# The second half of an ELU layer, recast in the form of the expert stage that follows it

## The chip, the cores and the metric

One core of one Trainium2 chip runs the whole kernel. The metric is device time in microseconds: the median of three runs before the change is 1423.83 us (1423.03 to 1424.04).

## The reference

Three layers follow each other on 2304 tokens of 512 numbers.

1. Linear attention over 4 batches x 8 heads x 576 tokens: features `exp(p)` and `exp(-p)` of a projection from which the largest absolute value was taken, two small matrix products, a division.
2. A feed-forward layer with ELU. Its inputs `w_in` and `w_out` come in 64-bit floating point:

```python
h = x @ w_in                                  # 512 -> 2048
g = where(h > 0, h, exp(minimum(h, 0)) - 1)
x = g @ w_out                                 # 2048 -> 512
```

3. Four experts of width 1024 on all tokens, weighted by normalised probabilities: `out += p[:, e] * (relu(x @ w1[e]) @ w2[e])`.

## The kernel before, in words

**Products.** To keep float32 precision, each factor is split into a high part and a remainder, and each product is three matmuls (high x high, high x remainder, remainder x high).

**Order of the work.** The kernel is written as Python generators that hand out instructions in program order; a planner (the tile framework, with a simulated time line) then orders each engine's instructions by program order and by when they become ready, and places the waits. A tile of a pool is waited for until all its earlier users are done. All DMAs go through SP's queue, in order.

**Attention** (lines 168 to 329) works on 16 pairs of heads, several in flight. While the ELU layer's first half runs, each `slot()` (line 718) hands out 1.4 attention steps and 2 steps of `weight_stream`. A `limit` and a `goal` keep attention some pairs ahead of the ELU token tiles.

**Weights of the ELU layer.** `convert64` (line 100) turns a 128 x 256 piece of 64-bit numbers into float32: two ScalarE passes, four VectorE passes, a GpSimd multiplication and a GpSimd addition, then the split into high part (ScalarE) and remainder (GpSimd), written to a ring of 16 tiles. There are 32 tiles of weights, 64 pieces. `conversions` (line 400) yields nothing while the ring has no room; tiles are released by the last of the nine token tiles.

**ELU layer.** `Elu` (line 512) is one unit: a token tile of 256 and two blocks of 128 hidden features. `l1` makes 24 matmuls of 256 columns, then ReLU of the negative, Exp, a combination, a copy and a subtraction; `l2`, one unit later, makes 24 matmuls into four accumulators. The 16 blocks of hidden features are done in two halves of eight: the first half runs over all nine token tiles (the last three interleaved, `TAIL`) and stores partial sums to DRAM (`x1scr`); the second half loads the tokens again from DRAM (`load_x`), loads the partial sums (`load_part`) and stores the sum (`x1fin`). Two matmuls of an unbroken queue of 24 look like this:

```python
PE.matmul(ph[:, j], w[:, 0, c], xh[:, kc], start=(kc == 0), stop=False)
PE.matmul(ph[:, j], w[:, 0, c], xl[:, kc], start=False, stop=False)
```

**Expert stage.** Tokens are taken in three groups of 2 x 384. The first product of an expert uses one level of Strassen's scheme: seven products instead of eight. `split_x1` (line 588) forms the seven token combinations, `weight_stream` (line 434 on) the seven weight combinations of each of four quarters. `Up` (line 622) has `begin`, `middle` and `end` per quarter: seven products of 6 matmuls of 384 columns, accumulated in three PSUM banks; ScalarE copies a bank (`keep`) before TensorE adds to it, VectorE adds the copies. `half` turns each of the four result blocks into a high part (ScalarE, line 653) and a remainder (VectorE, line 654). `Down` (line 685) is the second product, of 512 columns, one PSUM bank for 128 tokens; it scales and adds to sums kept in DRAM (`yscr`). One expert's weights take 14 + 8 ring tiles; the ring is 16 tiles plus 7 more (`ring2`) that are opened during the second ELU half, when the conversions are over.

## Time and profile before

| what | value |
|---|---|
| median of three runs | 1423.83 us |
| profiled execution | 1424.05 us |
| its span | 1422.3 us |
| TensorE busy | 1380.5 us, 8688 matmuls |
| VectorE / ScalarE / GpSimd busy | 698.2 / 619.9 / 446.7 us |
| granted TensorE clock, mean | 0.997 |

The span is the time from the first to the last instruction that the profiler recorded; all prices below come from this one execution. A busy TensorE need not be TensorE at its peak, since matmuls overlap: the distance from one matmul's start to the next one's tells more than a duration does. `L525` is line 525 of the kernel.

### The profile page before, as it was taken

The numbers are of one execution on the slowest core, as the hardware profiler recorded it, in microseconds if no ns is written. First come the engines' busy times: TensorE is split into PE (matmuls) and PEld (weight loads), VectorE is DVE, ScalarE is ACT, GpSimd is POOL, SyncE is SP. The second block draws the span as 40 slices with busy tenths as digits, with TensorE's granted clock in tenths as the row PEclk, the third lists the DMA queues.
The fourth block names the chain that finished last, engine by engine and source line by source line (L and its number), as shares of the span: only waits on it lengthen the run. The fifth ranks groups of instructions, "written<-read, shape, count | busy, mean of one in ns | idle before, by whom it ended". The sixth has DMA issues, their size and how long they took to land.

```text
span 1422.3 us, 22325 instructions
## 1 busy us (share of the span) xinstructions
PE 1380.5 (97%) x8688; PEld 1286.9 (90%) x8688; DVE 698.2 (49%) x1150; ACT 619.9 (44%) x1348; POOL 446.7 (31%) x499
## 2 busy tenths in 40 slices
PE   7889999999999999999999999999999999999998
PEld 6788999999988999998898989898888989899897
DVE  7998856575588534333434323234432325323332
ACT  6777776665656544343333443122421214322121
POOL 5567654434588512033102350002320004300000
PEclk9999999999999999999999999999999999999999
DMA  5433222120423345313333233434145251433421
GB/s 162 128 118 117 88 66 77 40 74 24 128 90 118 112 143 191 108 46 104 114 131 148 94 106 135 160 112 148 45 149 181 105 196 52 141 111 133 167 78 67
DMA packets 93625, 160.22 MB, mean 113 GB/s; under 512 B 28496, under 2 KB 39888, under 8 KB 93520
## 3 DMA queue, kind: packets, MB, share of 16 engines
q1 hardware_dynamic: 93520, 158.80, 33.7%
q8 instruction: 68, 1.11, 0.3%
q14 instruction: 37, 0.30, 0.1%
HBM read 109.22 MB, written 49.55 MB: 112 GB/s over the span
## 4 chain that ended last, share of the span: by engine, by line
PE 74%; DVE 11%; DMA 5%; POOL 4%; issue 3%; ACT 3%; SPq 0%; DVEq 0%; POOLq 0%; ACTq 0%
PE bank L701 8%; PE bank L702 8%; PE bank L703 8%; PE bank L642 8%; PE bank L643 7%; PE bank L644 7%; PE bank L555 3%; PE bank L556 3%; PE bank L554 3%; PE bank L527 3%; PE bank L525 3%; PE bank L526 3%; PE bank L237 2%; PE bank L316 2%; DMA wst<-in_w 2%
## 5 line engine op out<-in xcount | busy, mean ns | idle before, releaser
L701 PE MATMUL bank<-w,h 128*128 128x512 f32 x576 | 224.5, 392 | 4.0 <-ACT h L653 4.0
L642 PE MATMUL bank<-xv,w 128*128 128x384 f32 x672 | 224.3, 340 | 3.1 <-ACT cm L648 2.9
L643 PE MATMUL bank<-xv,w 128*128 128x384 f32 x672 | 226.6, 337 | 0.0
L702 PE MATMUL bank<-w,h 128*128 128x512 f32 x576 | 225.5, 392 | 0.0
L644 PE MATMUL bank<-xv,w 128*128 128x384 f32 x672 | 223.4, 338 | 0.0
L703 PE MATMUL bank<-w,h 128*128 128x512 f32 x576 | 198.3, 391 | 0.7 <-DVE h L654 0.7
L462 POOL TENSOR_TENSOR w<-wst,w 128x256 fp32r<-128x256 f32 x80 | 62.2, 796 | 341.0 <-ACT w L461 336.9
L555 PE MATMUL bank<-gl,w 128*128 128x256 f32 x576 | 162.3, 286 | 6.3 <-DVE gl L538 5.0
L556 PE MATMUL bank<-gh,w 128*128 128x256 f32 x576 | 160.9, 284 | 0.0
L554 PE MATMUL bank<-gh,w 128*128 128x256 f32 x576 | 156.3, 288 | 3.9 <-ACT gh L537 3.4
L642 PEld LDWEIGHTS bank<-xv,w 128*128 128x128 f32 x672 | 126.6, 188 | 11.1 <-ACT cm L648 3.5
L654 DVE SCALAR_TENSOR_TENSOR h<-bank,h 128x384 fp32r<-128x384 f32 x144 | 77.4, 554 | 115.1 <-ACT h L653 115.1
L653 ACT ACTIVATE h<-bank 128x384 fp32r<-128x384 f32 x144 | 66.8, 490 | 151.6 <-PE bank L644 91.7
L701 PEld LDWEIGHTS bank<-w,h 128*128 128x128 f32 x576 | 108.5, 188 | 25.1 <-ACT h L653 5.3
L643 PEld LDWEIGHTS bank<-xv,w 128*128 128x128 f32 x672 | 126.8, 189 | 4.4
L702 PEld LDWEIGHTS bank<-w,h 128*128 128x128 f32 x576 | 108.6, 189 | 20.6
L644 PEld LDWEIGHTS bank<-xv,w 128*128 128x128 f32 x672 | 126.3, 188 | 0.0
L703 PEld LDWEIGHTS bank<-w,h 128*128 128x128 f32 x576 | 107.3, 188 | 20.0 <-DVE h L654 1.6
L555 PEld LDWEIGHTS bank<-gl,w 128*128 128x128 f32 x576 | 110.1, 191 | 9.6 <-DVE gl L538 7.5
L554 PEld LDWEIGHTS bank<-gh,w 128*128 128x128 f32 x576 | 106.1, 191 | 6.8 <-ACT gh L537 6.5
L556 PEld LDWEIGHTS bank<-gh,w 128*128 128x128 f32 x576 | 110.1, 191 | 0.2
L648 ACT ACTIVATE cmab<-bank 128x384 f32<-128x384 f32 x48 | 23.6, 492 | 178.0 <-PE bank L644 178.0
(119 smaller groups left out, 2991.0 us busy)
## 6 DMA issues: line engine op xcount, KB each, us to landing
xv<-xvd SPq DMA_DIRECT2D x42, 768.0 KB, 4.4
wst<-in_w SPq DMA_DIRECT2D x64, 256.0 KB, 2.8
xvd<-xv SPq DMA_DIRECT2D x21, 768.0 KB, 4.4
yscr<-y SPq DMA_DIRECT2D x54, 256.0 KB, 2.3
y<-yscr SPq DMA_DIRECT2D x54, 256.0 KB, 2.9
w<-in_w_in SPq DMA_DIRECT2D x32, 256.0 KB, 2.8
w<-in_w_out SPq DMA_DIRECT2D x32, 256.0 KB, 3.0
kq<-in_kq SPq DMA_DIRECT2D x16, 320.0 KB, 3.0
```

The costliest lines, as they stand in the source:

```text
L462: on[WL[v % len(WL)]].tensor_tensor(out=lo, in0=x, in1=f32(hi), op=ALU.subtract)
L554: PE.matmul(o, w[:, 0, c], self.gh[:, j], start=start, stop=False)
L555: PE.matmul(o, w[:, 0, c], self.gl[:, j], start=False, stop=False)
L556: PE.matmul(o, w[:, 1, c], self.gh[:, j], start=False, stop=stop)
L642: PE.matmul(o, hi[:, c], x[:, 0, kc], start=not more and kc == 0, stop=False, skip_group_check=more)
L643: PE.matmul(o, hi[:, c], x[:, 1, kc], start=False, stop=False, skip_group_check=more)
L644: PE.matmul(o, lo[:, c], x[:, 0, kc], start=False, stop=kc == 1, skip_group_check=more)
L653: A.activation(h[:, 0], c, ACTF.Relu)
L654: V.scalar_tensor_tensor(out=h[:, 1], in0=c, scalar=0.0, in1=f32(h[:, 0]), op0=ALU.max, op1=ALU.subtract)
L701: PE.matmul(self.acc, h[:, 0, c], w[:, 0], start=f == 0, stop=False)
L702: PE.matmul(self.acc, h[:, 0, c], w[:, 1], start=False, stop=False)
L703: PE.matmul(self.acc, h[:, 1, c], w[:, 0], start=False, stop=f == 2 * NQ - 1)
```

## The change

The first half of the ELU layer stays as it is, with the last two token tiles interleaved instead of three. The second half takes the form of the expert stage, as an expert numbered -1:

- Its weights are still converted piece by piece, but right behind the first half's, and stored as float32 in DRAM (`wscr`); `weight_stream` later loads them like an expert's and forms the Strassen combinations and the splits. They take no ring tile until then.
- Its first product is `UpElu`, Strassen's scheme of `Up` with an ELU in `half`. Its tokens are loaded from DRAM in groups of 2 x 384 (`x_att`) and split by `split_x`.
- Its second product is `Out`: plain matmuls of 384 columns with the weights as the stationary operand, accumulated in four banks for 384 tokens; `drain` adds the first half's partial sums, loaded into `part` tiles, and stores to `x1fin`.
- The ring beside the main one has 6 tiles instead of 7, and pools move between the two sides of SBUF.

The diff, cut to its core:

```diff
-RING2 = 7
+RING2 = 6
...
-TAIL = 3
+TAIL = 2
+ATE = 6
+WFAST = 4
+TEB = 2
+PB = 4
+EL = 'V'
...
-    xscr = [[dram.tile([P, S], F32, name=f"xscr{b}_{p}") for p in range(NP)] for b in range(B)]
-    x1fin = [dram.tile([P, KD, TS], F32, name=f"x1fin{t}") for t in range(NTS)]
+    xscr = [dram.tile([P, NP, S], F32, name=f"xscr{b}") for b in range(B)]
+    wscr = {(nm, f): dram.tile([P, DM], F32, name=f"w{nm}{f}") for nm in ("in", "out") for f in range(FP, 2 * FP)}
+    x1fin = [[dram.tile([P, KD, TC], F32, name=f"x1fin{g}_{s}") for s in range(2)] for g in range(NG)]
...
-    p2 = ExitStack()
-    tmp = pool("tmp", stack=p2)
-    gt = pool("gt", LAG + 1, stack=p2)
...
         adder.tensor_tensor(out=f32(top), in0=f32(top), in1=low, op=ALU.add)
+        if dst.dtype == F32:
+            SP.dma_start(dst, f32(top))
+            return
         A.activation(dst[:, 0], f32(top), ACTF.Copy)
         yield
         G.tensor_tensor(out=dst[:, 1], in0=f32(top), in1=f32(dst[:, 0]), op=ALU.subtract)
...
+    tmp = pool("tmp", stack=right, side="right")
+    gt = pool("gt", LAG + 1, stack=right, side="right")
...
-        pl = ring2[0] if len(order_b) % (RING + RING2) < RING2 else ring
+        pl = ring if len(order_b) % (RING + RING2) < RING else ring2[0]
...
-        if ring2[0] is None or RING2 <= n < RING + RING2 and n - RING2 >= freed[0] - (len(users) - RING):
-            return False
-        return n - freed_b[0] < RING + RING2
+        if n < RING:
+            return n < freed[0]
+        return ring2[0] is not None and n - freed_b[0] < RING + RING2
...
-    def room():
-        return len(users) - freed[0] < RING
...
     def conversions():
-        for u in range(FP):
+        for u in range(FP // 2):
             for nm, src in (("in", w_in), ("out", w_out)):
                 for f in (2 * u, 2 * u + 1):
-                    while not room():
-                        yield None
                     ring_tile((nm, f))
                     for o in range(0, 512, CVW):
-                        yield convert64(rings[nm, f][:, :, o:o + CVW], src[f][:, o:o + CVW], G if f < CVP else V), (nm, f, o)
+                        yield convert64(rings[nm, f][:, :, o:o + CVW], src[f][:, o:o + CVW], G), (nm, f, o)
+        for nm, src in (("in", w_in), ("out", w_out)):
+            for f in FORDER:
+                for o in range(0, 512, CVW):
+                    yield convert64(wscr[nm, FP + f][:, o:o + CVW], src[FP + f][:, o:o + CVW], G), (nm, FP + f, o)
...
-        while ring2[0] is None:
+        while wst[0] is None:
             yield
-        for e in range(E):
...
-                    SP.dma_start(t, w1[e, f])
+                    SP.dma_start(t, w1[e, f] if e >= 0 else wscr["in", FP + f])
...
-                SP.dma_start(t, w2[e, f])
+                SP.dma_start(t, w2[e, f] if e >= 0 else wscr["out", FP + f])
...
+        def __init__(self, t, u):
+            self.t, self.u = t, u
             self.first, self.last = u == 0, u == FP // 2 - 1
-            self.fu = half * (FP // 2) + u
...
-            (V if self.half * NTS + self.t >= GLV else G).tensor_tensor(out=self.gl, in0=g, in1=f32(self.gh), op=ALU.subtract)
+            (V if self.t >= GLV else G).tensor_tensor(out=self.gl, in0=g, in1=f32(self.gh), op=ALU.subtract)
...
         def drain(self, acc):
-            t = self.t
             for a in range(2):
-                d = slice(2 * a, 2 * a + 2)
-                if self.half == 0:
-                    st = tmp.tile([P, 2, TS], F32, tag="xs", name="xs", bufs=2)
-                    A.activation(st, acc[a], ACTF.Copy)
-                    SP.dma_start(x1scr[t][:, d], st)
-                else:
-                    st = tmp.tile([P, 2, TS], F32, tag="xs", name="xs", bufs=2)
-                    V.tensor_tensor(out=st, in0=acc[a], in1=part[t][a], op=ALU.add)
-                    SP.dma_start(x1fin[t][:, d], st)
-
-    def load_half(g, s, kh):
-        x = xb.tile([P, 2, TC], F32, tag="xs", name="xs", bufs=XSB)
+                st = tmp.tile([P, 2, TS], F32, tag="xs", name="xs", bufs=2)
+                A.activation(st, acc[a], ACTF.Copy)
+                SP.dma_start(x1scr[self.t][:, 2 * a:2 * a + 2], st)
+
+    def pieces(i, size):
         o = 0
         while o < TC:
-            t, c = divmod((2 * g + s) * TC + o, TS)
-            n = min(TS - c, TC - o)
-            SP.dma_start(x[:, :, o:o + n], x1fin[t][:, 2 * kh:2 * kh + 2, c:c + n])
+            t, c = divmod(i * TC + o, size)
+            n = min(size - c, TC - o)
+            yield slice(o, o + n), t, slice(c, c + n)
             o += n
+
+    def x_att(g, s, kh):
+        x = xb.tile([P, 2, TC], F32, tag="xs", name="xs", bufs=XSB)
+        for o, b, c in pieces(2 * g + s, S):
+            SP.dma_start(x[:, :, o], xscr[b][:, 2 * kh:2 * kh + 2, c])
         return x
 
-    def split_x1(g):
+    def x_elu(g, s, kh):
+        x = xb.tile([P, 2, TC], F32, tag="xs", name="xs", bufs=XSB)
+        SP.dma_start(x, x1fin[g][s][:, 2 * kh:2 * kh + 2])
+        return x
...
+    def split_x(g, load_half, keep):
...
-            SP.dma_start(xvd[g][k], f32(xv))
+            if keep:
+                SP.dma_start(xvd[g][k], f32(xv))
...
-            c = hp.tile([P, TC], F32, tag=name, name=name, bufs=bufs)
+            c = (cmp if name == "cm" else hp).tile([P, TC], F32, tag=name, name=name, bufs=bufs)
...
+    class UpElu(Up):
+        def half(self, c, s, f):
+            h = hp.tile([P, 2, TC], F32R, tag="h", name="h", bufs=HB)
+            t = bp.tile([P, TC], F32, tag="te", name="te", bufs=TEB)
+            A.activation(t, c, ACTF.Relu, scale=-1.0)
+            A.activation(t, t, ACTF.Exp, scale=-1.0)
+            V.scalar_tensor_tensor(out=t, in0=t, scalar=1.0, in1=c, op0=ALU.subtract, op1=ALU.max)
+            A.activation(h[:, 0], t, ACTF.Copy)
+            on[EL].tensor_tensor(out=h[:, 1], in0=t, in1=f32(h[:, 0]), op=ALU.subtract)
+            hs[s, f] = h
+
+    class Out:
+        def __init__(self, g, s):
+            self.g, self.s = g, s
+            self.acc, self.part = {}, {}
+
+        def load(self, dc):
+            self.part[dc] = bp.tile([P, TC], F32, tag="part", name="part", bufs=PB)
+            for o, t, c in pieces(2 * self.g + self.s, TS):
+                SP.dma_start(self.part[dc][:, o], x1scr[t][:, dc, c])
+
+        def run(self, dc, qs):
+            if dc not in self.acc:
+                self.acc[dc] = bank()[:, :TC]
+            c = slice(dc * P, (dc + 1) * P)
+            o = self.acc[dc]
+            for q in qs:
+                for f in (q, q + NQ):
+                    w, h = rings["w2", -1, f], hs[self.s, f]
+                    PE.matmul(o, w[:, 0, c], h[:, 0], start=f == 0, stop=False)
+                    PE.matmul(o, w[:, 1, c], h[:, 0], start=False, stop=False)
+                    PE.matmul(o, w[:, 0, c], h[:, 1], start=False, stop=f == 2 * NQ - 1)
+
+        def drain(self, dc):
+            V.tensor_tensor(out=self.part[dc], in0=self.acc[dc], in1=self.part[dc], op=ALU.add)
+            SP.dma_start(x1fin[self.g][self.s][:, dc], self.part[dc])
...
-        for _ in range(WRATE):
+        for _ in range(wrate[0]):
...
-    def order(tail, skew):
+    def order(tail):
         seq = [(t, u) for t in range(NTS - tail) for u in range(HU)]
-        both = sorted([(u + skew * (t - NTS + tail), t, u) for t in range(NTS - tail, NTS) for u in range(HU)])
-        return seq + [(t, u) for _, t, u in both]
+        return seq + [(t, u) for u in range(HU) for t in range(NTS - tail, NTS)]
...
+    nxt = iter(())
+    for t, u in order(TAIL):
         if u == 0:
             goal = NP * ((TS * t + TS - 1) // S + 1)
             while done[0] < goal:
                 next(stream)
             limit[0] = NP * (t // 2 + 2)
-            rate[0] = RATE if t < 6 else 0.0
-            if t == 6:
+            rate[0] = RATE if t < ATE else 0.0
+            if t == ATE:
                 att.close()
-                s2 = pool("s2", 2, stack=p2)
+                xb = pool("xb")
+                wst[0] = pool("wst")
+                cmp = pool("cmp")
+                wrate[0] = WFAST
+            if t == NTS - TAIL:
+                nxt = split_x(0, x_att, False)
         need_w(("elu", u))
-        drive(Elu(0, t, u))
-        if t == NTS - 2 and u == 0:
-            load_x(0)
-    load_part(0)
-    for t, u in order(2, LAG):
-        if (t, u) == (GATE, 0):
-            for k in range(FP):
-                need_w(("elu", k))
-            right.close()
-            wst[0] = pool("wst", side="right")
-            ring2[0] = pool("ring2", RING2, side="right")
-            xb = pool("xb", side="right")
-        if u == 0 and t + 1 < NTS:
-            load_x(t + 1)
-        if u == LAG and t + 1 < NTS:
-            load_part(t + 1)
-        need_w(("elu", HU + u))
-        drive(Elu(1, t, u))
-        if (t, u) == (NTS - 1, XAT):
-            for _ in split_x1(0):
-                pass
-    norm_probs()
+        drive(Elu(t, u))
+        next(nxt, None)
+    for _ in nxt:
+        pass
+    wrate[0] = WRATE
+    need_w(("w1", -1, 0))
+    ups = [UpElu(-1, q, xcur[0][1]) for q in range(NQ)]
+    ups[0].begin()
     while pend:
         pend.pop(0).l2(slot)
-    p2.close()
+    right.close()
+    ring2[0] = pool("ring2", RING2, side="right")
     hp = pool("hp")
+    bstack = ExitStack()
+    bp = pool("bp", stack=bstack)
+    norm_probs()
+    for g in range(NG):
+        last = g == NG - 1
+        first, second = Out(g, 0), Out(g, 1)
+        for dc in range(KD):
+            first.load(dc)
+        if g:
+            ups = [UpElu(-1, q, xcur[0][1]) for q in range(NQ)]
+            ups[0].begin()
+        for q in range(NQ):
+            ups[q].middle()
+            slot()
+            if q:
+                for f in (q - 1, q - 1 + NQ):
+                    need_w(("w2", -1, f))
+                for dc in range(KD):
+                    first.run(dc, (q - 1,))
+                slot()
+            if q + 1 < NQ:
+                need_w(("w1", -1, q + 1))
+                ups[q + 1].begin()
+            ups[q].end()
+            if last and q % 2:
+                release_b(*(("w1", -1, q // 2, n) for n in range(7)))
+            slot()
+        nxt = split_x(0, x_elu, True) if last else split_x(g + 1, x_att, False)
+        need_w(("w2", -1, 2 * NQ - 1))
+        for dc in range(KD):
+            next(nxt, None)
+            second.run(dc, range(NQ - 1))
+            slot()
+        for dc in range(KD):
+            first.run(dc, (NQ - 1,))
+            first.drain(dc)
+            second.load(dc)
+            next(nxt, None)
+        slot()
+        for dc in range(KD):
+            second.run(dc, (NQ - 1,))
+            second.drain(dc)
+        if last:
+            release_b(*(("w2", -1, f) for f in FORDER))
+        for _ in nxt:
+            pass
+        slot()
+    bstack.close()
...
-            nxt = (fetch_x if steps[k + 1][0] else split_x1)(steps[k + 1][1])
+            nxt = fetch_x(steps[k + 1][1]) if steps[k + 1][0] else split_x(steps[k + 1][1], x_elu, True)
```

## Rows read from the trace of the kernel before

**Rows 1.** The page, part 1: busy time, share of the span, instructions.

```profile
PE 1380.5 (97%) x8688; PEld 1286.9 (90%) x8688; DVE 698.2 (49%) x1150; ACT 619.9 (44%) x1348; POOL 446.7 (31%) x499
```

**Rows 2.** The page, part 4: shares of the chain that ended last.

```profile
PE 74%; DVE 11%; DMA 5%; POOL 4%; issue 3%; ACT 3%; SPq 0%; DVEq 0%; POOLq 0%; ACTq 0%
```

**Rows 3.** Stretches: length; PE, PEld, DVE, ACT, POOL busy (instructions); clock, DMA share, GB/s.

```profile
100.00:150.00 50.00, 47.94 (x354) 44.96 (x355) 42.78 (x82) 36.74 (x89) 37.62 (x49) 1.00 0.39 121
105.00:365.00 260.00, 257.35 (x2100) 253.34 (x2098) 172.23 (x260) 175.69 (x398) 136.69 (x153) 1.00 0.24 74
375.00:475.00 100.00, 92.60 (x729) 88.19 (x728) 83.31 (x150) 63.65 (x148) 81.56 (x99) 1.00 0.33 104
400.00:450.00 50.00, 45.48 (x348) 42.28 (x347) 47.05 (x86) 33.04 (x78) 40.74 (x51) 1.00 0.33 111
475.00:550.00 75.00, 73.69 (x606) 72.69 (x606) 38.37 (x49) 33.79 (x55) 22.29 (x15) 1.00 0.52 176
655.00:675.00 20.00, 17.08 (x89) 15.68 (x88) 5.46 (x10) 4.86 (x10) 5.57 (x5) 0.83 0.22 75
700.00:850.00 150.00, 150.00 (x742) 134.21 (x741) 56.71 (x88) 60.19 (x123) 37.94 (x38) 1.00 0.35 123
850.00:900.00 50.00, 49.81 (x256) 45.62 (x255) 15.09 (x28) 13.83 (x30) 4.66 (x5) 1.00 0.37 130
985.00:1050.00 65.00, 61.35 (x303) 54.37 (x303) 30.99 (x50) 26.40 (x62) 29.99 (x34) 1.00 0.33 105
```

**Rows 4.** TensorE in order: start, duration, matmul, [idle before, releaser]; end of ELU.

```profile
659.73 0.28 PE L556 MATMUL bank<-gh,w 128*128 128x256 f32 x1
...
660.45 0.28 PE L556 MATMUL bank<-gh,w 128*128 128x256 f32 x1
...
662.48 0.45 PE L642 MATMUL bank<-xv,w 128*128 128x384 f32 x1 [1.75 <-ACT cm L648]
...
665.01 0.69 PE L642 MATMUL bank<-xv,w 128*128 128x384 f32 x1 [1.17 <-ACT cm L648]
```

**Rows 5.** TensorE in order, inside one quarter of expert 0.

```profile
735.67 0.33 PE L642 MATMUL bank<-xv,w 128*128 128x384 f32 x1
...
738.13 0.34 PE L644 MATMUL bank<-xv,w 128*128 128x384 f32 x1
```

**Rows 6.** Groups by line: shapes, count, busy us, mean ns, idle before; conversion pieces.

```profile
L110 DVE TENSOR_SCALAR top<-top 128x256 f32<-128x256 f32 x64 | 26.3, 418 | 12.4 <-ACT top L108 12.1
...
L111 DVE TENSOR_SCALAR top<-top 128x256 uint32<-128x256 uint32 x64 | 30.1, 477 | 0.9
...
L112 DVE SCALAR_TENSOR_TENSOR top<-w,top 128x256 uint32<-128x256 uint32 x64 | 39.6, 625 | 0.9
...
L113 DVE TENSOR_SCALAR pw<-top 128x256 uint32<-128x256 uint32 x64 | 25.8, 411 | 0.9
...
L108 ACT ACTIVATE top<-w 128x256 f32<-128x256 f32 x64 | 27.2, 433 | 13.0 <-POOL w L121 11.7 <-DMA w<-in_w_in 1.1
...
L116 POOL TENSOR_TENSOR low<-low,pw 128x256 f32<-128x256 f32 x64 | 50.5, 791 | 46.8 <-DVE pw L113 46.8
```

**Rows 7.** GpSimd and ScalarE in order of time, 143 to 316 us.

```profile
144.02 0.79 POOL L121 TENSOR_TENSOR w<-top,w 128x256 fp32r<-128x256 f32 x1
...
314.72 0.60 ACT L533 ACTIVATE g<-bank 128x512 f32<-128x512 f32 x1 [0.73 <-PE bank L527]
```

**Rows 8.** Groups by line: the experts' blocks after the first matmul.

```profile
L653 ACT ACTIVATE h<-bank 128x384 fp32r<-128x384 f32 x144 | 66.8, 490 | 151.6 <-PE bank L644 91.7 <-DVE bank L683 45.0 <-DVE bank L666 13.1
...
L654 DVE SCALAR_TENSOR_TENSOR h<-bank,h 128x384 fp32r<-128x384 f32 x144 | 77.4, 554 | 115.1 <-ACT h L653 115.1
...
L654 DVE SCALAR_TENSOR_TENSOR h<-c,h 128x384 fp32r<-128x384 f32 x48 | 34.0, 709 | 26.8 <-ACT h L653 26.4
```

**Rows 9.** Waits: who waited for whom, us in total, times, longest.

```profile
DVE y L711 <- DMA y<-yscr: 35.9, 16, 6.6
```

More of the change, by code (lines that the diff above doesn't have):

```diff
@@ L418, in weight_stream @@
                     more = False
[L419 removed]
+                else:
                     live.append(g)
@@ L432, in weight_stream @@
                 yield
-        while ring2[0] is None:
+        while wst[0] is None:
             yield
-        for e in range(E):
+        for e in range(-1, E):
             for q in range(NQ):
@@ L484, in attn_elu_moe_kernel @@
     stream = attention()
[L485 to L486 removed]
     accs = {}
     count = [0]
[L490 to L510 removed]
     class Elu:
[L513 to L514 removed]
+        def __init__(self, t, u):
+            self.t, self.u = t, u
             self.first, self.last = u == 0, u == FP // 2 - 1
[L516 removed]
         def l1(self, slot):
[L519 removed]
+            xh, xl = xt[self.t]
             ph = bank((P, 2, TS))
             for j in range(2):
[L522 removed]
+                w = rings["in", 2 * self.u + j]
                 for kc in range(KD):
@@ L547, in l2 @@
             for j in range(2):
-                w = rings["out", 2 * self.fu + j]
+                w = rings["out", 2 * self.u + j]
                 for dc in range(KD):
@@ L748, in attn_elu_moe_kernel @@
             next(weights)
-    s2 = None
-    for t, u in order(TAIL, 0):
+    nxt = iter(())
+    for t, u in order(TAIL):
         if u == 0:
```

40 lines of the change are left out of this document (5 added, 35 removed).

## The prediction

> **What bounds the kernel now.** I read the busy table first: TensorE is busy for 1380.5 of 1422.3 us, VectorE for about half of that [rows 1]. The chain that ended last is 74% TensorE and 11% VectorE [rows 2]. So nearly the whole span is a TensorE queue, and a change is worth two things: matmul time it removes, and places where TensorE stands still. The table of stretches [rows 3] says where those places are. From 700 to 850 us TensorE is busy for all 150 us; from 105 to 365 us, where attention and the first half of the ELU layer run side by side, it loses 2.65 of 260 us. It loses between 375 and 550 us, about the junction of the two ELU halves, between 655 and 675 us, where the ELU layer hands over to the experts, and a little where experts change (985 to 1050 us).
>
> A full queue of this kind has a price per matmul, read from starts that follow each other without a break: six matmuls of 256 columns from 659.73 to 660.45 us, 120 ns each [rows 4]; 14 of 384 columns from 735.67 to 738.13 us, 175.7 ns each [rows 5].
>
> **1. Matmuls removed and added.** The second ELU half has 9 token tiles x 4 units x 48 = 1728 matmuls of 256 columns: 1728 x 0.120 = 207.4 us. In its place stand, for each of 3 groups of 768 tokens, 4 quarters x 7 Strassen products x 6 = 168 matmuls and 2 x 4 x 8 x 3 = 192 plain ones, all of 384 columns: 1080 x 0.1757 = 189.8 us. TensorE saves 17.6 us. It is on the path, and nothing hides it.
>
> The Trainium skill (page "TensorE: Matmul & The Clock Gate", section "Back-to-back issue gap") gives a gap of N/2.4 ns plus 2.5 ns at full clock. By it the two streams cost 188.7 and 175.5 us and the saving is 13.2 us. The rows above show 13.3 and 15.7 ns over N/2.4 for both shapes in this kernel, so the measurement decides.
>
> **2. The conversions of the second half's weights move forward.** Each of the 64 pieces costs VectorE 0.418 + 0.477 + 0.625 + 0.411 = 1.93 us, ScalarE two passes of about 0.43 us and a third as long, and GpSimd 0.79 us three times [rows 6]. Today the later 32 pieces wait for ring tiles, which come free only in the last token tile of the first half. Now they go to DRAM; they skip the last ScalarE copy and GpSimd subtraction and add a store. SP issues that store when GpSimd's addition is done, and loads queued behind it on SP, kq among them, wait with it.
>
> *What goes.* From 375 to 475 us TensorE starts 729 matmuls, all but a few of 256 columns, in 100 us: at 0.120 us that is 87.5 us, so 12.5 us are lost. From 475 to 550 us 606 make 72.7 of 75 us, 2.3 lost [rows 3]. Together 14.8 us.
>
> *What comes.* Counting the steps that each slot hands to the weight stream (2 a slot, 4 slots a unit, 4 steps a piece), the 32 pieces take 16 units from the end of the first half's conversions (144.0 us) to the unit of token tile 4 that starts its ELU at 314.7 us [rows 7]: about 170 us. VectorE is already busy for 172.2 of 260 us there, 66%, and 62 us more are 36%: it comes close to full. Bounds: no loss, since attention and the ELU units feed TensorE alternately and nobody waits for these conversions; or the rate of 400 to 450 us, where VectorE is busy for 47 of 50 us and TensorE starts 348 matmuls of 256 columns (41.8 us, 8.2 lost): 170/50 x 8.2 = 28 us. The row nearest in kind is 100 to 150 us, with attention, ELU and conversions together and VectorE at 42.8 of 50: 2.06 us idle, 7 us in 170. I take 8.
>
> The end of the first half keeps its ELU chains and gets the token split and the first Strassen weights in place of the conversions. Its own loss I take from 475 to 550 us: 2 us (0 to 6). Part 2: -14.8 + 8 + 2 = -4.8 us.
>
> **3. The junction to the Strassen form.** Between 655 and 675 us TensorE is idle for 2.9 us, and the granted clock is 0.83, which at two levels means 6.8 us at 1.2 GHz and 3.4 us of work lost; the fall comes behind a wait of 1.75 us for the copy of the first product, and a second of 1.17 us follows [rows 3, 4]. This junction goes: -6.3 us. The new one sits at the end of the first half. There the first product is written before the last ELU unit's 24 matmuls (2.9 us), which cover the copy; its weights need ring tiles that are free some 25 us earlier. I take 2.5 us, between 0 and the old 6.3. Part 3: -3.8 us.
>
> **4. Waits inside the 12 quarters.** Each of the 48 half-blocks now takes three ScalarE passes and two VectorE passes (ReLU, Exp, one combination, copy, subtraction) where an expert's takes one and one. By the rows of the experts' blocks [rows 8] that is 3 x 0.49 + 0.55 + 0.71 = 2.7 us of chain. Per quarter ScalarE has 15 passes, 7.4 us, in about 11 us of matmuls. TensorE needs ScalarE only for the copies that free a bank before it adds to it; the combination's wait is queued on VectorE ahead of the quarter's additions. The experts' quarters lose nothing between 700 and 850 us, and the plain matmuls of the previous quarter lie ready beside. Bounds 0 and 12 x 1 us; I take 0.3 us each: +3.6 us.
>
> **5. Group changes and a new expert boundary.** In the plain matmul's drains the second half-group's partial sums are loaded into the tiles that the first's have just been stored from, so VectorE can stand in front of a load. This happens today with y: 35.9 us in 16 waits [rows 9], and it is why the expert change from 985 to 1050 us idles 3.65 us, while the one from 850 to 900 us idles 0.19. The ELU stage is one more expert: two group changes (0 to 1.8 us each, 0.5 taken) and a boundary (0.2 to 3.65, 2 taken): +3 us.
>
> **6. One ring tile fewer.** 22 tiles hold exactly one expert's weights (14 + 8), so the next one can't begin a tile early. Three boundaries at 0 to 1 us, +1 us together.
>
> **Sum.** -17.6 - 4.8 - 3.8 + 3.6 + 3 + 1 = -18.6 us. The profiled execution took 1424.05 us (span 1422.3); it becomes 1405.4. The median shown is 0.2 us lower: 1405 us. Taking the good end of every part gives about 1387, the bad ends about 1445, but they don't fall together.
>
> **Rivals.**
>
> *A. VectorE fills up beside attention (slower).* Place: 145 to 315 us. If each of the 170 us loses as 400 to 450 us does (28 us), part 2 is 20 us worse and the time 1425; since here attention's own chain runs through VectorE as well, up to 34 us and 1431. It decides from a loss of 27 us, 16% of the stretch. For it: 66% + 36% is over what VectorE has. Against: TensorE loses nearly nothing there now, and the conversions may slide into later gaps. Chance 0.12.
>
> *B. The longer chain shows in the quarters.* If banks run out (four accumulators, two products, two halves in the chain), TensorE waits a good part of 2.7 us a quarter; at 1 us it is 12 instead of 3.6 and the time 1414, at 1.5 us 1420, at the full chain 1434. For it: all eight banks are used. Against: a bank given up in one quarter is wanted about 3 us later. Chance 0.10.
>
> *C. The boundaries are dear.* 3.65 us at each of three changes instead of 3 in all, and the half clock of the old junction returns once (3.4 us): 11 us more, 1416. For it: loads of partial sums, weights and tokens share one queue. Against: the experts' first group changes are free. Chance 0.10.
>
> *D. Better than that.* The conversions cost nothing and the junction less: 1391 to 1394. Chance 0.06.
>
> *E. A smaller price per matmul.* If a matmul cost only its columns at 2.4 GHz, 442,368 columns would give way to 414,720, 184.3 us to 172.8, and part 1 would be 11.5 us: 1411. Against it stand 14 starts in a row at 175.7 ns [rows 5]. Chance 0.02. The Trainium skill's figure (the page and section named in part 1) would put this case at 1410.
>
> **How the numbers follow.** The forecast, 1405, has 0.60, with its own range of 1394 to 1414. Less than 0.2% (2.8 us) can't be told from no change. Faster: 0.60 + 0.06 (D) + 0.02 (E) + 0.10 (C) + 0.06 of B = 0.84. Same: 0.03 of A and 0.02 of B = 0.05. Slower: 0.09 of A and 0.02 of B = 0.11. The range 1391 to 1423 leaves out A, the end of B and the end of D.
>
> **What would show it.** Part 1: 1080 matmuls of 384 columns in the ELU stage at 176 ns, no 256-column ones after the first half. Part 2: VectorE near 95% between 145 and 315 us, conversions over before 330 us, TensorE's idle time there under 10 us, and the stretch of 100 us before the Strassen form losing about 2 us rather than 12.5. Part 3: no stretch at half clock at the end of the ELU layer. Part 4: waits of TensorE for the copies in the quarters, under 4 us in sum. Part 5: VectorE waiting for loads of partial sums at two group changes. The prediction is wrong if the first half ends more than 8 us later than it would by these losses, if the 189.8 us of the new stage stretch beyond 200 us, or if the half clock returns at the new junction.

## The result, and the profile after

The changed kernel takes 1438.41 us (median of 4 runs, 1436.79 to 1443.22) against 1423.93 us for the kernel before on the same chip: ratio 1.0107, 95% interval 1.0081 to 1.0132. It is 1% slower; the forecast was 1405 us. The changed kernel's profiled span is 1436.1 us, 13.8 us over before's.

The page of the changed kernel, part 1 (busy time, share, instructions), answers to [rows 1]:

```profile
PE 1376.5 (96%) x8040; PEld 1271.6 (89%) x8040; DVE 751.3 (52%) x1253; ACT 644.1 (45%) x1436; POOL 448.9 (31%) x506
```

648 matmuls have gone, and TensorE is busy only 4 us less in a longer span. VectorE works 53 us more. That is the new stage's own work: the VectorE passes of the pieces (a piece is 128 x 256 numbers of a weight, the unit of a conversion) were there before too.

Three last matmuls cut the span into segments. Attention's starts at 353.5 us before and 384.7 after: 31.2 us later. The ELU layer's starts at 660.5 and 670.7: from attention's end the change *gains* 21.0 us. The experts' last starts at 1416.7 and 1431.2: the expert stage is 4.3 us longer. The tail gives 0.7 back. 31.2 - 21.0 + 4.3 - 0.7 = 13.8.

The changed kernel's table of stretches (length; PE, PEld, DVE, ACT, POOL busy and instructions; clock, DMA share, GB/s), the first four for the place to which the conversions moved, the fifth for the time right behind them, the others to set beside [rows 3]:

```profile
145.00:310.00 165.00, 142.59 (x1104) 138.22 (x1103) 141.45 (x239) 110.09 (x260) 116.88 (x136) 0.95 0.40 124
...
150.00:200.00 50.00, 42.48 (x322) 41.17 (x321) 45.61 (x75) 31.88 (x79) 37.10 (x43) 0.93 0.43 135
200.00:250.00 50.00, 46.41 (x363) 44.91 (x363) 45.27 (x76) 35.68 (x83) 36.96 (x43) 0.97 0.40 127
250.00:300.00 50.00, 39.77 (x307) 38.51 (x306) 41.42 (x74) 31.37 (x75) 33.55 (x40) 0.93 0.39 121
300.00:350.00 50.00, 50.00 (x421) 49.77 (x420) 32.66 (x49) 34.59 (x76) 21.62 (x24) 1.00 0.21 65
...
375.00:475.00 100.00, 98.17 (x798) 97.45 (x796) 51.04 (x64) 53.86 (x109) 40.58 (x45) 1.00 0.30 93
...
475.00:550.00 75.00, 70.94 (x389) 68.87 (x387) 40.73 (x67) 38.83 (x80) 14.24 (x9) 0.98 0.28 87
655.00:675.00 20.00, 18.57 (x106) 18.25 (x105) 9.78 (x16) 6.62 (x13) 8.30 (x7) 1.00 0.59 194
```

The kernel before in the first of these windows:

```profile
145.00:310.00 165.00, 163.32 (x1355) 161.98 (x1354) 104.34 (x151) 113.87 (x254) 86.29 (x91) 1.00 0.23 69
```

Read both by their counts: TensorE starts 1104 matmuls in 165 us, where it started 1355. By the traces the 251 missing ones are 165 of 256 columns (120 ns each in a full queue), 50 of 128 (112 ns) and 36 of 288 (133 ns), together about 30 us: nearly the whole delay at attention's end. Two things make up most of it. TensorE is idle for 165 - 142.59 = 22.4 us, and the mean granted clock of 0.95 means about 17 us at the lower of its two levels, 1.2 GHz. As soon as the pieces are over (300 to 350) TensorE is busy without a break. From 375 to 475 us 1.8 of 100 us are idle, where before 7.4 were, and at the end of the ELU layer the clock is full.

Who stopped TensorE there: the changed kernel's waits of PE, 145 to 310 us (us in total, times, longest):

```profile
PE bank L248 <- DVE qd L209: 13.7, 6, 8.3
PE bank L200 <- DVE g L514: 3.6, 1, 3.6
PE bank L533 <- POOL gl L516: 2.6, 3, 1.1
PE bank L532 <- ACT gh L515: 1.3, 1, 1.3
```

17.3 of 22.4 us are waits for VectorE, none of them for a conversion's result. It is attention's own query features (qd) and an ELU unit's g that come late. What VectorE did in the 10 us up to the stop for g, which lasted from 181.47 to 185.06 us:

```profile
175.26 0.99 DVE L109 TENSOR_SCALAR top<-top 128x256 f32<-128x256 f32 x2
176.17 0.28 DVE L112 TENSOR_SCALAR pw<-top 128x256 uint32<-128x256 uint32 x1
176.37 1.05 DVE L110 TENSOR_SCALAR top<-top 128x256 uint32<-128x256 uint32 x2
177.34 2.36 DVE L111 SCALAR_TENSOR_TENSOR top<-w,top 128x256 uint32<-128x256 uint32 x2
179.63 0.48 DVE L112 TENSOR_SCALAR pw<-top 128x256 uint32<-128x256 uint32 x2
180.03 1.94 DVE L329 RECIPROCAL rc<-rc 128x288 f32<-128x288 f32 x1
181.89 0.62 DVE L208 TENSOR_REDUCE mx<-bank 128x4 f32<-128x512 f32 x1
182.44 1.93 DVE L329 RECIPROCAL rc<-rc 128x288 f32<-128x288 f32 x1
184.29 0.62 DVE L514 SCALAR_TENSOR_TENSOR g<-g,bank 128x512 f32<-128x512 f32 x1
```

Not one conversion pass (L109 to L112) stands in the stop itself; 4.8 us of them stand right before it, and attention's and the ELU unit's work follows behind. The longest stop, first on TensorE, then what VectorE did in it (start, duration, instruction, [idle before, releaser]):

```profile
263.94 0.29 PE L202 MATMUL bank<-wbl,sh 128*128 128x256 f32 x1
272.58 1.09 PE L248 MATMUL bank<-ident,qd 128*128 128x128 f32 x4 [8.35 <-DVE qd L209]
```

```profile
264.46 0.29 DVE L109 TENSOR_SCALAR top<-top 128x256 f32<-128x256 f32 x1 [0.87 <-ACT top L107]
264.83 1.95 DVE L329 RECIPROCAL rc<-rc 128x288 f32<-128x288 f32 x1
266.70 0.23 DVE L109 TENSOR_SCALAR top<-top 128x256 f32<-128x256 f32 x1
266.85 0.93 DVE L332 TENSOR_TENSOR xf<-bank,rc 64x288 f32<-64x288 f32 x2
267.81 0.29 DVE L110 TENSOR_SCALAR top<-top 128x256 uint32<-128x256 uint32 x1
268.13 1.29 DVE L208 TENSOR_REDUCE mx<-bank 128x4 f32<-128x512 f32 x2
...
270.88 0.29 DVE L109 TENSOR_SCALAR top<-top 128x256 f32<-128x256 f32 x1
271.09 0.29 DVE L110 TENSOR_SCALAR top<-top 128x256 uint32<-128x256 uint32 x1
271.29 0.42 DVE L111 SCALAR_TENSOR_TENSOR top<-w,top 128x256 uint32<-128x256 uint32 x1
271.74 1.29 DVE L209 TENSOR_TENSOR qd<-bank,mx 128x512 f32<-128x512 f32 x2
```

Reciprocals, maxima and products of attention stand in one queue with conversion passes (L109 to L111), three of them right ahead of the qd that TensorE waits for, and one that itself stood 0.87 us for ScalarE. But in the 8.35 us, counted from each start to the next, these passes fill 1.6 us, attention's and the ELU unit's own work 6.3. Over all stops from 145 to 310 us (22.3 us) it is 6.0 us of conversion passes and 15.7 of the other work. The run without the pieces (e1, below) has no stops there, so most of the delay arose before the stop in which it shows: VectorE was already behind. Behind these two long stops TensorE comes back at the lower clock. The changed kernel's TensorE behind the stop of 3.59 us:

```profile
185.06 0.55 PE L200 MATMUL bank<-wbh,sh 128*128 128x256 f32 x1 [3.59 <-DVE g L514]
185.41 0.41 PE L201 MATMUL bank<-wbh,sl 128*128 128x256 f32 x1
...
186.26 0.41 PE L202 MATMUL bank<-wbl,sh 128*128 128x256 f32 x1
```

Four gaps from 185.41 to 186.26 us, 0.85 us: 212 ns a matmul instead of 120, at a granted clock of 0.50 (186 to 190 us). Of the 17 us at the lower level 4.6 lie inside the stops; in the other 12.5 TensorE worked, which cost 12.5 x (1 - 120/212) = 5.4 us. With 22.4 us idle that makes 27.8 of the 30; most of the rest stands in slow first matmuls behind a stop, such as 0.35 us to the next start at 185.06. The forecast's figure for this place was 8 us.

The new stage itself, from the changed kernel's groups by line and its waits of VectorE; the last line answers to [rows 9]:

```profile
L696 PE MATMUL bank<-h,w 128*128 128x384 f32 x192 | 65.7, 344 | 7.2 <-DVE te L673 6.4 <-ACT h L674 0.8
```

```profile
DVE y L729 <- DMA y<-yscr: 45.3, 14, 9.0
...
DVE part L701 <- DMA part<-x1scr: 17.1, 10, 5.6
```

TensorE waits 6.4 us for the ELU combinations at the plain matmuls, and about 3 us elsewhere in the stage; VectorE stands 17.1 us in front of loads of partial sums, which TensorE hardly feels.

### The profile page after: what moved, and what is told of

It is laid out like the page before. It is cut to its first block, busy times and chain, and to the rows that moved or that the text cites. A ratio compares the mean times of both kernels' runs of the same rounds, so it can differ in the third digit from the quotient of the medians.

```text
span 1436.1 us, 21373 instructions
## 1 busy us (share of the span) xinstructions
PE 1376.5 (96%) x8040; PEld 1271.6 (89%) x8040; DVE 751.3 (52%) x1253; ACT 644.1 (45%) x1436; POOL 448.9 (31%) x506
## 4 chain that ended last, share of the span: by engine, by line
PE 64%; DMA 3%; DVE 3%; ACT 1%; issue 1%; POOL 1%; SPq 0%; DVEq 0%; POOLq 0%; ACTq 0%
PE bank L623 9%; PE bank L624 9%; PE bank L625 9%; PE bank L719 9%; PE bank L721 9%; PE bank L720 9%; PE bank L696 2%; PE bank L697 2%; PE bank L698 2%; DMA wst<-in_w 1%; PE bank L533 1%; PE bank L534 1%; PE bank L532 1%; DMA y<-yscr 1%; PE bank L504 1%
## 5 line engine op out<-in xcount | busy, mean ns | idle before, releaser
L623 PE MATMUL bank<-xv,w 128*128 128x384 f32 x840 | 279.3, 337 | 6.0 <-DVE c L656 2.8
L624 PE MATMUL bank<-xv,w 128*128 128x384 f32 x840 | 281.6, 335 | 0.0
L625 PE MATMUL bank<-xv,w 128*128 128x384 f32 x840 | 277.3, 335 | 0.0
L465 POOL TENSOR_TENSOR w<-wst,w 128x256 fp32r<-128x256 f32 x100 | 76.7, 787 | 383.9 <-ACT w L464 368.9
L623 PEld LDWEIGHTS bank<-xv,w 128*128 128x128 f32 x840 | 157.7, 188 | 17.5 <-DVE c L656 3.1
L624 PEld LDWEIGHTS bank<-xv,w 128*128 128x128 f32 x840 | 157.8, 188 | 4.8
L625 PEld LDWEIGHTS bank<-xv,w 128*128 128x128 f32 x840 | 157.4, 188 | 0.0
L720 PEld LDWEIGHTS bank<-w,h 128*128 128x128 f32 x576 | 108.1, 188 | 22.3
L574 POOL TENSOR_TENSOR xv<-xs,xv 128x768 fp32r<-128x768 f32 x24 | 46.1, 1925 | 192.1 <-ACT xv L573 184.2
L647 DVE TENSOR_TENSOR bank<-cm,bank 128x384 f32<-128x384 f32 x60 | 33.6, 560 | 131.6 <-PE bank L625 117.8
L656 DVE TENSOR_TENSOR c<-cmab,bank 128x384 f32<-128x384 f32 x60 | 33.2, 553 | 126.1 <-ACT cmab L629 126.0
L629 ACT ACTIVATE cm<-bank 128x384 f32<-128x384 f32 x60 | 29.4, 490 | 136.4 <-PE bank L625 136.4
L533 PE MATMUL bank<-gl,w 128*128 128x256 f32 x288 | 81.9, 288 | 4.0 <-POOL gl L516 2.6
L503 PE MATMUL bank<-xh,w 128*128 128x256 f32 x288 | 83.2, 290 | 0.4 <-DVE qd L209 0.4
```

What stands on the lines that cost most here:

```text
L465: on[WL[v % len(WL)]].tensor_tensor(out=lo, in0=x, in1=f32(hi), op=ALU.subtract)
L533: PE.matmul(o, w[:, 0, c], self.gl[:, j], start=False, stop=False)
L623: PE.matmul(o, hi[:, c], x[:, 0, kc], start=not more and kc == 0, stop=False, skip_group_check=more)
L624: PE.matmul(o, hi[:, c], x[:, 1, kc], start=False, stop=False, skip_group_check=more)
L625: PE.matmul(o, lo[:, c], x[:, 0, kc], start=False, stop=kc == 1, skip_group_check=more)
L629: A.activation(c, ps, ACTF.Copy)
```

## The experiments

All are the changed kernel with one edit. The diffs are cut to the lines that matter, and what stands behind `#` in them is added here. Times stand beside the kernel before on the same chip (medians 1422.96 to 1425.44 us). "Attention's end" is the start of its last matmul: 353.5 us before, 384.7 after.

**e1, e2, e3: which part of the moved conversions costs.**

```diff
 e1: -        for nm, src in (("in", w_in), ("out", w_out)):   # the later 32 pieces; expert 0's weights are loaded
 e2: -            SP.dma_start(dst, f32(top))                  # only the store; expert 0's weights are loaded
 e3: +        if dst.dtype == F32:                             # loads, two ScalarE passes and stores stay
     +            A.activation(low, lo, ACTF.Copy, scale=2.0 ** -52)
     +            SP.dma_start(dst, f32(top))
     +            return
```

e1 leaves out the conversion of the second half's weights, e2 its stores, e3 its VectorE and GpSimd passes.

> Leaves out the conversion of the second half's weights (the new stage loads expert 0's weights in their place); all else as in the changed kernel. Attention's last matmul came at 353.5 us before and at 384.7 us in the changed kernel. All theories: the loss beside attention goes, attention ends at 352 to 356 us, and the time is 1438 - 31 = 1407 us (1404 to 1412). If attention still ends after 365 us, its delay is not from these conversions but from the other edits (pools, pacing, queue order).

> Leaves out only the 32 stores of converted pieces to DRAM (the new stage loads expert 0's weights); every ScalarE, VectorE and GpSimd pass stays. Theory T1 (VectorE's added 62 us, its queue nearly full): nothing changes beside attention, which ends at 380 to 385 us, time 1435 to 1439. Theory T2 (ScalarE, and behind it VectorE, stand in front of the store's completion before they may write the tile again, and SP's queue holds loads behind a store): attention ends by 360 us, time 1410 to 1416. T3 (half and half): about 1424.

> Keeps loads, two ScalarE passes and the stores of the 32 pieces, leaves out their four VectorE and two GpSimd passes (the stored numbers are not the converted ones). T1: attention ends by 360 us, time 1407 to 1414. T2: attention ends at 375 us or later, time 1430 to 1438.

Measured: e1 1401.23 us (ratio 0.9843, 0.9814 to 0.9871), attention's end 352.3. e2 1437.9 (1.0100, 1.0071 to 1.0130), end 383.7. e3 1411.4 (0.9914, 0.9885 to 0.9943), end 357.3. The stretch 145 to 310 us of e1, then of e3:

```profile
145.00:310.00 165.00, 165.00 (x1375) 164.02 (x1374) 100.71 (x141) 112.07 (x249) 82.54 (x87) 1.00 0.22 67
```

```profile
145.00:310.00 165.00, 160.32 (x1322) 158.04 (x1322) 96.37 (x137) 126.45 (x301) 79.80 (x84) 1.00 0.43 134
```

Without the pieces TensorE is never idle there, and the time is 22 us below that of the kernel before (3 us below e1's range of 1404 to 1412). So the pieces cost 37 us in all (36 if each run is set against the kernel before on its own chip), 32 of them by attention's end (384.7 - 352.3), not the 8 forecast. Without the stores the time falls by 0.5 us, less than the spread of the runs: queued loads on SP are not the cause. With loads and stores but no VectorE and GpSimd passes 27 of the 37 us are gone. Theory T1 of e2 and e3, VectorE, held in both.

**e6: VectorE or GpSimd.**

```diff
+        if dst.dtype == F32:          # the two GpSimd passes of these 32 pieces are left out
+            yield
+            SP.dma_start(dst, f32(top))
+            return
         G.tensor_tensor(out=low, in0=low, in1=f32(pw), op=ALU.mult)
```

> Leaves out the two GpSimd passes of the 32 DRAM pieces (so the stored numbers lack their low words' part); loads, ScalarE passes, the four VectorE passes and the stores stay. The 31 us by which attention ends later hang on VectorE or GpSimd passes (without both it ended at 357 us). VectorE theory: attention ends at 372 us or later, time 1426 to 1438. GpSimd theory: attention ends by 364 us, time under 1418. In between the two share it.

Measured: 1434.86 us (1.0068, 1.0048 to 1.0088), attention's end 379.8; the VectorE theory held. Taking away one thing after the other: GpSimd's passes 3.5 us (the three runs of e6 lie 5 us apart), VectorE's 23.5 (1434.9 to 1411.4), loads, ScalarE passes and stores 10.2 (1411.4 to 1401.2). Most of the cost is VectorE's four passes.

**e5, e9, e11: is it the density?** e5 halves the steps per slot in tiles 1 to 5; e9 ties each piece to an ELU unit by data; e11 puts the tie behind the piece's load. In e9 and e11 the faster rate of 4 steps begins with the last two token tiles.

```diff
 e5:  +            if 0 < t < ATE:
      +                wrate[0] = 1
 e9:  +        if dst.dtype == F32 and unit_gh[0] is not None:   # ahead of the load; 1.25 steps a slot
      +            A.activation(st.bitcast(F32)[:, :1], f32(unit_gh[0])[:, 0, :1], ACTF.Copy)
 e11: +            A.activation(f32(top)[:, :1], f32(unit_gh[0])[:, 0, :1], ACTF.Copy)   # ahead of the first pass; 1.6 steps
```

> All work stays; each slot hands out one step of the weight stream instead of two while token tiles 1 to 5 run, so that the 32 conversions stretch to about 400 us. T1 (too much VectorE work in 150 us): VectorE's share beside attention falls from 90% to near 80%, attention ends at 360 to 368 us, the last conversions cost a few us behind it, time 1418 to 1426. T2 (each store blocks): the same 32 waits at other places, attention ends at 370 us or later, time over 1428.

> All work stays. Before each DRAM piece's load a one-column ScalarE copy from the latest ELU unit's tile is written into the piece's tile, so that the planner can't start a piece before that unit; slots hand out 1.25 steps in token tiles 1 to 6. The pieces stand between 150 and about 400 us instead of 145 and 302. Theory (VectorE's queue is too full from 150 to 300 us, 45 of 50 us busy, and the planner pulls ready conversions forward whatever the slots say): VectorE is at 40 to 42 of 50 us, TensorE idles under 2 us in 50, attention ends at 356 to 364 us, time 1408 to 1418, faster than before. Rival (the conversions' passes cost TensorE the same wherever they stand beside attention): attention ends at 375 us or later, time 1432 to 1440.

> As e9 (each piece of a conversion tied to an ELU unit by a one-column ScalarE copy, so that the 32 pieces spread from 147 to 420 us), but the copy is written into the piece's top tile ahead of its first pass, not into its load tile ahead of the load: the load is then in place when ScalarE comes to the pass. Theory U (e9's pieces still cost 23 us by the end of attention because ScalarE, in order, stands behind passes that wait for their loads: 11.8 us of such waits in 150 to 310 us): those waits go below 3 us, attention ends at 366 to 371 instead of 375.1, the time is 1424 to 1430. Rival V (the passes themselves, standing in VectorE's and ScalarE's order ahead of attention's own, cost it wherever they stand): attention ends at 374 to 378, the time is 1431 to 1435. Simple fullness of VectorE would give neither, since VectorE is at 74 to 83 per cent there in e9.

Measured: e5 1438.83 us (1.0107, 1.0067 to 1.0146). Its pieces stand within 1.3 us of where they stood: the slots set no pace, so e5 says nothing on density, and its time fits T2's range for no reason of T2's. The reading that fits e9's ties is that the planner pulls whatever is ready forward; every step of a conversion is also handed out under `tc.high_priority(offset=CVOFF)` with `CVOFF = 0` (line 423 of the kernel before), and no run changed that. e9 1432.61 (1.0063, 1.0043 to 1.0082), attention's end 375.1, pieces from 147 to 419 us. e11 1435.76 (1.0070, 1.0055 to 1.0085), end 378.2. The stretch 145 to 310 us of e9, then ScalarE's waits of e9 (145 to 365 us):

```profile
145.00:310.00 165.00, 152.88 (x1236) 149.53 (x1234) 129.10 (x202) 115.36 (x278) 103.57 (x116) 0.99 0.33 103
```

```profile
ACT top L112 <- DMA w<-in_w_in: 11.8, 6, 3.0
...
ACT top L112 <- DMA w<-in_w_out: 8.6, 5, 2.8
```

VectorE is down to 78% (it was 86% in after, 61% in e1), and TensorE is still idle for 12 us of 165 there and for more behind. The gain is 6 us where e9's theory (VectorE's queue too full) had 20 to 30; its rival's ranges, 375 us or later and 1432 to 1440, held. e11 took most of those waits away (145 to 310 us: 2.7 us for loads, 14.9 in e9) and brought nothing, so theory U fell, while V's range for attention's end (374 to 378) was missed by 0.2 and that for the time by 0.8: spread over 270 us the 32 pieces of e9 still cost 31 of the 37 us that they cost in 155. What is not separated: the ties are themselves instructions on ScalarE and part of this price, so e9 and e11 don't show what the passes alone cost at this spread.

**e13, e14: the pieces behind attention.** As e9's tie, with the pieces held until token tile 6 (e13, four steps a slot) or 5 (e14, two and then four), and e10's ring (below).

```diff
+        while tok[0] < ATE:           # e14: ATE - 1
+            yield None, None
```

> The weights' place as in e10, and the 32 pieces held back until all of attention has been issued (each tied by a one-column ScalarE copy to an ELU unit of token tiles 6 and later), four steps per slot: so they stand beside the last third of the ELU layer's first half, where the kernel before had its last 28. Theory V (a piece costs about 1 us beside attention however it is spread, 33 of 32 in after, 29 in e9, because its passes stand in VectorE's order ahead of a chain with many hops; beside the ELU matmuls alone, where a unit has few hops, it costs about 0.5, as 14.8 us for 28 in the kernel before): attention ends at 352 to 356, the 32 pieces cost 15 to 18 us, the time is 1410 to 1416, below the kernel before. Rival W (a piece costs 1 us wherever it stands): 1430 to 1434. Rival X (32 pieces, the splitting of the first up weights and the splitting of the tokens no longer fit into the 100 us between attention and the new stage): the new stage waits at its start for weights, 8 to 20 us, and the time is 1418 to 1432 with an early end of attention.

> As e13, but the pieces are let go one token tile earlier (tile 5, two steps per slot, then four), so some begin beside attention's last two reciprocals. Theory V: some 8 of 32 stand beside attention's end and cost 1 us instead of 0.5, the time is 1413 to 1420; rival X: better than e13 by 4 to 10 us, since the new stage's weights are ready earlier; rival W: as e13, 1430 to 1434.

Measured: e13 1455.52 us (1.0231, 1.0214 to 1.0248), e14 1443.13 (1.0134, 1.0114 to 1.0153); both expectations failed. Attention's end comes at 351.2 in e13, 0.8 us ahead of theory V's range, and at 356.0 in e14, but in e13 the first half ends at 490.9 us instead of 469. e13's stretch, its waits of PE and of ScalarE, 375 to 490 us:

```profile
375.00:475.00 100.00, 68.76 (x429) 65.12 (x428) 80.04 (x152) 51.02 (x138) 68.10 (x82) 0.78 0.51 161
```

```profile
PE bank L546 <- ACT gh L528: 27.0, 8, 6.4
```

```profile
ACT w L105 <- DVE top L116: 25.4, 22, 4.1
```

The tie (L105) waits on ScalarE for VectorE to be done with the tile's last piece, and the ELU unit's gh stands behind it; TensorE stops up to 6.4 us and runs at a mean clock of 0.78. This run tells more about the tie than about the passes: whether 32 pieces could stand there at 0.5 us each, as before's later ones did, stays open.

**e8, e10, e12: the experts' price.** In a long stream without a break (below) the 512-column matmuls start 226.9 ns apart before and 232.7 after. By the order of the pools in the two kernels, two operands had moved from the low to the high end of the partition: the stationary h, and six of eight tiles of the moving w2. e8 puts two of h's 13 tiles low again, e10 all of w2; e12 is e10 with e11.

```diff
 e8:  +  h = hl.tile(..., bufs=2) if (s, f) in ((0, 0), (0, NQ)) else hp.tile(..., bufs=HB - 2)   # hl: a low pool
 e10: -  pl = ring if len(order_b) % (RING + RING2) < RING else ring2[0]
      +  n = len(order_b)
      +  pl = ring2[0] if 8 <= n % (RING + RING2) < 14 and n >= RING + RING2 or RING <= n < RING + RING2 else ring
      +  if RING + RING2 + 8 <= n < RING + RING2 + 14 and freed_b[0] < RING + RING2:   # in room_b: e0's last up tiles wait
      +      return False
```

> Two of the 13 h tiles (first token half, quarter 0) move from about 155 KiB to 80 KiB of a partition, the others stay; nothing else changes. In the changed kernel each expert matmul of 512 columns takes 232 ns instead of 228 ns, start to start. Theory P (it depends on where the h tile lies that is the weights of that matmul): the two tiles' matmuls (quarter 0 of the first token half) fall to about 228 ns, all others stay at 232 to 233 ns. Rival Q (another cause, as the order or the moving w tiles): all stay at 232 to 233 ns.

> The tile order of the ring is changed for the experts, so that their down weights (w2, the moving operand of the 512-column matmuls) lie in the 16 low tiles of the ring as in the kernel before, and six of the fourteen tiles of up weights in the second ring at the high end of the partition; e0's last six up tiles can then be taken only when the ELU layer's last matmul is done. Theory Q (the price of a 512-column matmul follows the place of its moving tile: 227.9 ns start to start before, all low; 233.2 for the high tiles and 230.4 for the low ones after): the 1728 matmuls return to 227 to 229 ns, the expert stage is 6 to 8 us shorter, about 1431 us in all. Rival R (the price follows something else of the new stage, such as the order of the program or what runs beside): they stay at 231 to 233 ns and the time stays at 1437 to 1439. Rival S (the up weights, as the stationary operand, take the price over): the 512-column ones fall and the 384-column ones rise from 174.0 towards 178, and 2 us are left of it. A late e0 shows as a VectorE or ScalarE wait of PE in the first 60 us of e0.

> e10 and e11 in one. If the two causes are separate, their gains add: U and Q 1417 to 1424 (below the kernel before), V and Q 1424 to 1428 (level with it), R and U 1424 to 1430, R and V 1431 to 1435.

Measured: e8 1436.23 us (one run): its matmuls with low h start 231.2 ns apart, and the same matmuls of after, with high h, 231.2; theory P's 228 fell. These are quarter 0's, whose two w2 tiles lie low in after already, so the place of h was tried with a low moving tile alone. e10 1432.5 (1.0051, 1.0034 to 1.0067). A run of 49 matmuls in the last expert, first and last start, of before, after and e10:

```profile
1343.46 0.40 PE L703 MATMUL bank<-w,h 128*128 128x512 f32 x1
...
1354.35 0.39 PE L703 MATMUL bank<-w,h 128*128 128x512 f32 x1
```

```profile
1357.33 0.40 PE L721 MATMUL bank<-w,h 128*128 128x512 f32 x1
...
1368.50 0.40 PE L721 MATMUL bank<-w,h 128*128 128x512 f32 x1
```

```profile
1350.95 0.39 PE L724 MATMUL bank<-w,h 128*128 128x512 f32 x1
...
1361.87 0.39 PE L724 MATMUL bank<-w,h 128*128 128x512 f32 x1
```

48 gaps in 10.89, 11.17 and 10.92 us: 226.9, 232.7 and 227.5 ns. Inside after's stream the six matmuls that by the program's order read the two low tiles stand out (first, fourth and the one behind the sixth):

```profile
1358.26 0.39 PE L719 MATMUL bank<-w,h 128*128 128x512 f32 x1
...
1358.96 0.39 PE L719 MATMUL bank<-w,h 128*128 128x512 f32 x1
...
1359.64 0.40 PE L719 MATMUL bank<-w,h 128*128 128x512 f32 x1
```

Their gaps are 232, 233, 230, 227, 227 and 226 ns; from the third one behind them on the gaps alternate between 229 and 237 or 238. After three low matmuls the price of before is back. Theory Q holds for the price (mean of the 512-column gaps 227.9 before, 232.5 after, 228.6 in e10), and S in part, since the 384-column ones rise from 174.0 to 175.2 ns. But the expert stage is not 6 to 8 us shorter: 759.7 us from the ELU layer's last matmul, against 760.6. 1728 x -3.9 ns = -6.7 us, 2016 x 1.2 ns = +2.4, +1.5 for a stretch of half clock at e0's start, and about +1.9 for longer stops, among them 1.6 us for e0's first down weight. Most of e10's 5.9 us came elsewhere: the new stage is 195.5 us long instead of 199.9 (e12: 195.9), with 4.3 instead of 6.4 us of waits for te at the plain matmuls and no half clock. The edit also keeps e0's last up weights from being prepared beside that stage; that this is the reason was not tried by itself.

e12 1430.31 us (1.0035, 1.0020 to 1.0050), between the ranges given for R with U and R with V: the ring again gives some 5.5 us on e11. No version with the conversions in it beats the kernel before.

## Why the prediction was wrong

- **Step 2, "What comes ... I take 8", failed.** By attention's end 31.2 us had come instead of 8. With 31.2 in its place the forecast would have been 1428; the other 9 to 10 us to 1438 came behind attention (last point). The place and the size were those of rival A, which had a chance of 0.12: its 28 to 34 us hold the 31.2, and only its time, up to 1431, was short, by those later terms. VectorE's added work was forecast rightly, 62 us against 63.7 in the trace. What failed is the step from that work to TensorE's loss.
- That step went by busy share. The choice between 0 and 28 went to the row "nearest in kind", 100 to 150 us, in which pieces, attention and ELU ran together [rows 3]. Its rate of pieces was no lower (12 in 50 us by the trace; the moved ones came at 9 to 11), and VectorE had 7.2 us free in it. In after it had 4.4, 4.7 and 8.6 us free in the three stretches of 50 us from 150 to 300, and TensorE was idle for 7.5, 3.6 and 10.2: the stretch with the freest VectorE lost the most. Part 2's own sign, VectorE near 95%, did not come (86% from 145 to 310 us). Attention was in another phase in the row: the groups by line show 6 of each matmul of L196 to L198 there and 18 in the 50 us behind it. That this phase makes the difference was not tried.
- What the price by busy share lacked was, by the trace, the order: VectorE works its queue front to back, and passes nobody is waiting for stood ahead of work that TensorE then needed, mostly well before the stop in which it shows. This is argued. e3 and e6 show that it is VectorE's passes, e9 that a price of 31 us remains at 78% of VectorE with its ties in it; no run changed the order alone.
- "The conversions may slide into later gaps" (against rival A) was wrong: in e5, where fewer steps were handed out, they stood where they had stood. That they would be over before 330 us was right (the last VectorE pass starts at 302 us).
- *What goes*, 14.8 us, held: counted by starts as there, 375 to 475 us loses about 2.5 instead of 12.5.
- **Step 1** held: the new stage's matmuls start 174 to 176 ns apart. The figure that part 1 and rival E set beside it, N/2.4 plus 2.5 ns, is by the Trainium skill ("TensorE: Matmul & The Clock Gate", section "Back-to-back issue gap") that of an isolated matmul, so these streams should not have been priced by it.
- **Step 3** held at the old place. At the new one TensorE waits 0.76 us (475.98) where 2.5 were forecast.
- **Step 4** was short: 9.7 us of waits in the new stage instead of 3.6, 7.5 of them for the combinations (te); the copies, for which it had priced the waits, took 1.4. Behind one wait for te (1.79 us at 483.10) the half clock returned for 3.4 us, in the stage's first quarter; the stage takes 199.9 us, just under its named limit of 200.
- **Steps 5 and 6**: group changes were nearly free, and VectorE's 17.1 us in front of loads cost TensorE nothing to speak of. The expert stage's 4.3 us more are another thing, which no step had: the price of a 512-column matmul changed with the place of its moving tile (1728 x 4.6 ns = +7.9 us), while the 384-column ones fell (2016 x -1.6 ns = -3.2), for which no run shows the reason.
- From attention's end on the forecast had -26.6 us to the end; it was -17.4. The 9.2 us between them lie in the new stage and in the experts.

## What to carry to other kernels

Here the price of work moved "beside" a busy stage did not follow the free share of the engine that it joined. Ask whose queue it joins and what stands behind it there: look for the product that the bound engine waits for, and count the moved instructions that can be put ahead of it. If an instruction is ready early, a planner may issue it early; a slower hand-out of steps is no pace, and a tie by data is itself an instruction that waits in order. Leave-one-out runs (no pieces, no stores, no passes) settled in three kernels which engine it was, where arguing from busy shares went wrong.

## What the runs showed of the hardware

The mean start-to-start price of the same 128x512 matmul was 227.9 ns with all moving tiles low (before), 230.4 for the low and 233.2 for the high ones of after, and 228.6 with all of them low again (e10). The low ones of after stand in short groups; in the group shown the first three still cost 230 to 233 ns, the next three 226 to 227. With low moving tiles the place of the stationary operand made no difference (231.2 and 231.2 ns for the same matmuls of e8 and after). One thing stays open: in before these matmuls, which stand in short groups among 384-column ones, cost 229.9 ns, and in e10 231.0, so neither edit brings that price back in full. Why place matters is not settled.

The Trainium skill ("SBUF — State Buffer", section "SBUF: two separate sides") says that on the engines' side only the port pair that VectorE and GpSimd share causes contention, and that TensorE waits for no one. These runs show a price of TensorE that depends on place; whether anything contends there no run shows.

The stops of 3.59 and 8.35 us on TensorE were each followed by work at the lower clock level (212 ns for a 256-column matmul), so about a fifth of the loss beside attention, 5.4 of 27.8 us, is not in any table of waits.
